# A graph layer that sorts its edges: GpSimd's gathers in another order, and three smaller edits

## The chip, the cores and the metric

The kernel runs on one core of a Trainium2 chip. The metric is device time in microseconds (us), the median of three timed runs of one launch. TensorE (PE), VectorE (DVE), ScalarE (ACT), GpSimd (POOL) and SyncE (SP) each run their own instruction stream in order and wait for one another by semaphores.

## The reference

One GraphSAGE layer over N = 12500 nodes with D = 64 features and E = 800000 random edges:

```python
nsum = _segment_sum(x[src], dst, N)
h_neigh = nsum * deg_inv[:, None]
return x @ w_self + h_neigh @ w_neigh
```

Every edge adds the feature row of its source node to its destination node; the sums are scaled per node and go through two 64x64 matrices.

## The kernel before, in words

The kernel doesn't gather 800000 feature rows. It sorts the edges by a key made of a destination group and a source group, and lets TensorE do gather and scatter with one-hot matrices.

**Keys and first sort.** Each of the 128 partitions takes 6250 edges, packs source and destination into one 32-bit key (`make_keys`) and sorts its run with a comb sort (`sort_runs`). A stage is a DVE minimum and a DVE maximum over pairs (L229), and ACT copies the elements that have no partner (L231). The first stages run over the whole run, the last 36 in three pieces, low, middle and high, so that the low part of each run is final first.

**Features.** Beside the sort `prepare` loads the features `x` (98 blocks of 64 per partition, 6272 values), takes their largest magnitude (`y`, L527 on ACT, L529 on DVE), derives a power of two from it through a small chain on DVE and PE (`e`, `ei`, `sc`, `scl`), and splits each scaled feature into a high part in 16 bits (`xh[..0]`, L552) and a low part (`xh[..1]`: the difference on DVE, L553, and its scaling on ACT, L554). `self_terms` multiplies the features with `w_self` (`xs`, `os`). This code is put in order by a scheduler; what follows stands in program order (`manual_schedule` in `after_sort`).

**Redistribution.** The 128 runs have to be cut at key boundaries and brought to 128 rows of a second level, in two parts (0 and 1). `find_rows` counts in each run how many keys lie below each row's first key: one instruction per row, on ACT (L374) or on DVE (L376). From the counts come start indices `ix`, and `gather_runs` has POOL issue one indirect DMA per run (`u<-d,ix`, L393), each followed by one (part 0) or two (part 1) short memsets of `pad` (`pause`, L306). Each row then holds 128 short sorted runs, and `merge_runs` merges them: first the near stages inside blocks of 32 runs (L415 the first stage of a block, L455 the others, L420 the copies on ACT; the tuple `blocks` says which blocks share an instruction), then `joined` and the far stages over all of them. Block 3 needs the last 32 gathers.

**Windows.** `find_and_gather` counts in the merged rows (L599, L601), and POOL gathers one window of each bucket (`v<-d,ix`, L605); `decode_buckets` turns the windows into source numbers (`sl`, through memory) and destination numbers (`dlT`). Edges that no window holds are leftovers: `leftovers` makes lists of them, and later `uses` says from which block on each list is due.

**Tiles.** 7644 buckets ("blocks") are summed, 8 per tile, 74 tiles per group of output nodes (`OCT` = 6 node blocks of 98 buckets, 588 blocks). For each tile PE does 8 matmuls `ct<-xh,ohs` (L852, gather by one-hot), ACT or DVE copies `ct` to `xg` (L862, L860), and PE does 16 matmuls `acc<-ohd,xg` (L907, scatter by one-hot). DVE makes the one-hots for 28 blocks at a time (`ohs` L823, `ohd` L826), some tiles ahead of PE. A leftover list takes an indirect DMA on POOL (`lx<-xt,lsrc`, L871, five buffers), a one-hot on DVE (`ohl`, L879) and a matmul into `acc` (L887); `rest` issues the DMA up to 160 blocks ahead.

**What is woven in.** Part 1 follows behind part 0. Its 128 run gathers are spread: 64 (`FIRST`) during the merges of part 0, 32 (up to `THEN`) at the end of `sums_and_merge`'s slots, and the last 32 (`runs`) one at every second tile. Its near merges run from tile 8 on, its block 3 and far stages from tile `RESUME` = 80 on, at a pace of 420 ns (`PACE`) per tile; all of them stand in DVE's order between the one-hots. POOL's order mixes the run gathers, the `lx` gathers and the output DMAs (L978) as the tiles come.

Of the kernel before, what the change touches and what calls it, by code (L numbers as in the profile page):

```python
# [22 lines left out]
NB = 98  # L23
# [21 lines left out]
EDGE = 32  # L45
PAUSE = (1, 2)
FIRST = 64
THEN = 96
EXT = 31
SIDE = H + EXT  # L50
# [3 lines left out]
BIG = float(np.array(BIGBITS, np.uint32).view(np.float32))  # L54
SIG = 5.5
AHEAD = 44
RESUME = 80
PACE = 420
SHARE = 503
SHARED = 60  # L60
# [200 lines left out]
class Kernel:  # L261
# [242 lines left out]
    def prepare(self, xp, mps):  # L504
# [19 lines left out]
        nc.sync.dma_start(dg[fd:fd + 1, :N - fd * FB], self.I["deg_inv"][fd * FB:].unsqueeze(0))  # L524

        y = xp.tile([128, NB, D], F32, name="y")
        nc.scalar.activation(y, x, AF.Abs)  # L527
        m = xp.tile([128, 1], F32, name="m")
        nc.vector.tensor_reduce(m, y.rearrange("p b f -> p (b f)"), axis=mybir.AxisListType.X, op=OP.max)  # L529
        ps = mps.tile([128, 128], F32, name="mps", tag="ct", bufs=3)  # L530
        nc.tensor.transpose(ps[:1], m, self.idf)
        e = xp.tile([1, 1], F32, name="e")
# [20 lines left out]
        nc.vector.scalar_tensor_tensor(y, x, scl[:, :1], self.xh[:, :, 0], op0=OP.mult, op1=OP.subtract)  # L553
        nc.scalar.activation(self.xh[:, :, 1], y, AF.Copy, scale=2048.0)  # L554
        nc.sync.dma_start(self.xt.rearrange("(b p) f -> p b f", p=128), self.xh.rearrange("p b a f -> p b (a f)"))

        nc.scalar.activation(y, x, AF.Abs, scale=scl[:, :1])
        z = xp.tile([128, NB, D], BF, name="z")
# [236 lines left out]
    def uses(self):  # L795


        out = []
        for o in range(0, NBID, OCT * NB):
            end = min(o + OCT * NB, NBID)  # L800
            here = []
            for p in range(2):
                for c in range(64):
                    lo = max(o, BASE[p] + c * 2 * KPRS[p])
                    hi = min(end, BASE[p] + (c + 1) * 2 * KPRS[p])
                    if hi > lo:
                        here.append([max(hi + 56, 380 + 24 * c) if p == 0 else hi + 56, p, c, lo // NB, (hi - 1) // NB])
            at = end + 8
            for use in sorted(here)[::-1]:
                at = use[0] = min(use[0], at - 24)  # L810
            out += sorted(here)
        return out
# [16 lines left out]
    def nodes(self, pool, aps, mps):  # L829
# [34 lines left out]

        def rest(b0):

            if len(picked) < self.used + 5 and len(picked) < len(uses) and uses[len(picked)][0] - 160 <= b0 \
                    and uses[len(picked)][1] in self.left:
                _, p, c, _, _ = uses[len(picked)]
                x = pool.tile([128, 128], FH, name="lx", bufs=5)  # L870
                nc.gpsimd.indirect_dma_start(  # L871
                    out=x, out_offset=None, in_=self.xt,
                    in_offset=bass.IndirectOffsetOnAxis(ap=self.left[p][1][:, c:c + 1], axis=0))
                picked.append(x)
                self.picked = len(done)
            if len(ohl) < len(picked) and len(ohl) < self.used + 5 and uses[len(ohl)][0] - 96 <= b0:
                _, p, c, first, end = uses[len(ohl)]
                m = pool.tile([128, 4 * HN], FH, name="ohl", bufs=5)
                nc.vector.tensor_scalar(m[:, :(end + 1 - first) * 2 * HN], self.wide[:, :(end + 1 - first) * 2 * HN],  # L879
                                        self.left[p][0][:, c:c + 1], -float(first * 2 * HN),  # L880
                                        op0=OP.subtract, op1=OP.is_equal)
                ohl.append(m)
            while self.used < len(uses) and uses[self.used][0] <= b0:
                _, p, c, first, end = uses[self.used]
                m = ohl[self.used].rearrange("p (b h n) -> p b h n", h=2, n=HN)
                for h in range(2):
                    nc.tensor.matmul(acc[h][:, first % OCT * HN:(first % OCT + end + 1 - first) * HN],  # L887
                                     picked[self.used], m[:, :end + 1 - first, h], start=False, stop=False)
                self.used += 1
# [167 lines left out]
    def after_sort(self, es, mps, aps):  # L1057
# [5 lines left out]
        with tc.manual_schedule():  # L1063
# [22 lines left out]
            sync.dma_start(self.d1[1], self.runs[:, UPPER1:])  # L1086
            self.l1ab.close()
            rows = self.find_rows(1, mps)
            for _ in range(SHARED):
                next(rows)  # L1090
            ways = None
            for i, _ in enumerate(self.merge_runs(0, u0, other, ((0, 2), (2, 1), (3, 1)))):
                if rows and [next(rows, None) for _ in range(2 - i % 2)][-1] is None:
                    rows = None
                    self.l1b.close()
                    self.gather_runs(1, u1, range(FIRST))
# [8 lines left out]
                    next(ways, None)  # L1105
            for _ in ways:
                pass
            self.store_rows(1, sync)
            self.sums_and_merge(es, mps, aps, u1, other, l2, l2b, l2a, va, vp)

    def sums_and_merge(self, es, mps, aps, u1, other, l2, l2b, l2a, va, vp):
# [11 lines left out]
        for slot in range(at[-1] + 2):  # L1123
            t += SLOT
            if ways and next(ways, None) is None:
                ways = None
                self.gather_runs(1, u1, range(FIRST, THEN))
            if slot < KPRS[0] - NLOWER and not on_act2(0, NLOWER + slot):
                t -= 750
            if slot in at or slot - 1 in at:  # L1130
# [16 lines left out]
        for n in self.nodes(fin, aps, mps):  # L1147
            if left and n >= left_at:
# [4 lines left out]
                        self.check(fin, mps)  # L1153
                else:
                    left_at = n + wait
            if runs and n % 2:
                self.gather_runs(1, u1, [runs.pop(0)])
            if tail and n % 2:
                next(tail, None)
# [55 lines left out]
```

## Time and profile before

| | |
|---|---|
| median of 3 timed runs | 1911.4 us (1903.02 to 1920.62) |
| the profiled execution's own time | 1896.69 us |
| its span, first to last instruction | 1895.0 us |
| busy: DVE, ACT, PE, POOL | 1677.9, 1166.8, 962.2, 841.8 us |
| first tile's one-hots on DVE | from 806.25 us on |

The profile is of one execution. Busy times are shares of one span, but the kernel has stages with different limits, so the stages are read one by one: the sort (to about 348 us), the gathers of part 0 (to about 552 us), its merges and windows (to about 806 us), and the tiles. In a row of the timeline the first number is the start, the second the duration; brackets hold the idle time of the engine before it and what ended it. A row of the windows view has a stretch, its length, and the busy time and count of the chosen instructions.

### The profile page before, as it was taken

How to read it: one execution, taken by the hardware profiler on the slowest of the kernel's cores; microseconds unless marked ns; L12 is line 12 of the kernel's file. 1: busy time of each engine (PE TensorE's matmuls, PEld its weight loads, DVE VectorE, ACT ScalarE, POOL GpSimd, SP SyncE). 2: the span in 40 equal slices, each digit the busy share in tenths (PEclk: the TensorE clock that was granted, in tenths of full speed). 3: DMA queues.
4: the chain of work that ended last, by engine and by line, in shares of the span. 5: the costliest groups of instructions: out<-in, count | busy, mean ns of one | idle time of the engine just before them, and what ended most of it. 6: DMA issues, size and time to landing. Idle time of an engine off the chain costs nothing.

```text
span 1895.0 us, 54521 instructions
## 1 busy us (share of the span) xinstructions
PE 962.2 (51%) x23659; PEld 838.7 (44%) x23659; DVE 1677.9 (89%) x1778; ACT 1166.8 (62%) x1835; POOL 841.8 (44%) x917
## 2 busy tenths in 40 slices
PE   0033000000000000083788887988979999889987
PEld 0023000000000000073677776777768788778886
DVE  7999999997749999795699999998998898888885
ACT  7463019305510022574689888988988887788786
POOL 1000000599889984798737322204662232322421
PEclk9985555555555555587899999999999999999998
DMA  4322000001100012274577877779867888888874
GB/s 152 70 63 73 0 24 8 25 20 52 22 20 10 10 38 70 82 283 137 185 230 246 256 244 251 251 258 312 285 223 250 270 276 257 269 272 278 272 252 147
DMA packets 104804, 305.24 MB, mean 161 GB/s; under 512 B 52945, under 2 KB 60491, under 8 KB 103915
## 3 DMA queue, kind: packets, MB, share of 16 engines
q1 hardware_dynamic: 86347, 277.44, 41.5%
q0 software_dynamic: 17632, 22.17, 8.7%
q8 instruction: 187, 3.06, 0.6%
q10 hardware_dynamic: 576, 2.07, 0.3%
q14 instruction: 62, 0.51, 0.1%
HBM read 282.20 MB, written 19.41 MB: 159 GB/s over the span
## 4 chain that ended last, share of the span: by engine, by line
DVE 40%; PE 24%; POOL 18%; issue 11%; DMA 3%; ACT 3%; DVEq 0%; SPq 0%; ACTq 0%; POOLq 0%
DVE u L455 14%; PE ct L852 13%; POOL u L393 13%; PE acc L907 9%; DVE a L229 7%; DVE b L229 7%; DVE ohd L826 5%; DVE ohs L823 4%; POOL pad L306 3%; POOL lx L871 2%; ACT xg L862 2%; DMA slb<-sl 1%; PE po L970 1%; DMA rd<-dst 1%; PE acc L887 1%
## 5 line engine op out<-in xcount | busy, mean ns | idle before, releaser
L862 ACT ACTIVATE xg<-ct 128x1024 f16<-128x1024 f32 (+1 forms) x898 | 856.4, 1043 | 188.6 <-PE ct L852 167.1
L852 PE MATMUL ct<-xh,ohs 128*128 128x128 f16 x7644 | 540.3, 224 | 69.7 <-DVE ohs L823 36.2
L852 PEld LDWEIGHTS <-ohs 128*128 128x128 f16 x7644 | 449.4, 100 | 110.0 <-issue 51.3
L393 POOL DMA_INDIRECT u<-d,ix x256 | 369.4, 1443 | 217.0 <-DVE ix L385 175.3
L907 PE MATMUL acc<-ohd,xg 64*128 64x80 f16 x15288 | 399.9, 200 | 58.9 <-issue 40.5
L455 DVE TENSOR_TENSOR u<-u 128x1456 f32<-128x1456 f32 (+46 forms) x292 | 394.5, 1378 | 6.6
L871 POOL DMA_INDIRECT lx<-xt,lsrc x140 | 265.6, 1897 | 249.1 <-PE acc L887 213.1
L907 PEld LDWEIGHTS <-xg 64*128 64x128 f16 x15288 | 318.4, 96 | 126.2 <-issue 57.4
L826 DVE TENSOR_TENSOR ohd<-iota,dlT 128x2240 f16<-128x2240 bf16 x273 | 360.3, 1320 | 0.0
L823 DVE TENSOR_SCALAR ohs<-slb,pidx 128x3584 f16<-128x3584 bf16 x273 | 314.6, 1152 | 37.4 <-PE ct L852 25.7
L383 PE MATMUL stp<-idf,st 128*128 128x128 f32 x2 | 0.9, 446 | 356.7 <-DVE st L381 356.7
L229 DVE TENSOR_TENSOR a<-b 128x608 f32<-128x608 f32 (+44 forms) x124 | 173.9, 1445 | 4.6
L229 DVE TENSOR_TENSOR b<-a 128x608 f32<-128x608 f32 (+44 forms) x124 | 173.9, 1444 | 4.3
L978 POOL DMA_DIRECT2D out<-o x25 | 22.8, 913 | 319.7 <-DVE o L977 245.5
L383 PEld LDWEIGHTS stp<-idf,st 128*128 128x128 f32 x2 | 0.4, 182 | 357.2 <-issue 357.2
L662 PE MATMUL tr<-idb,l 128*128 128x128 bf16 x60 | 8.0, 273 | 262.2 <-ACT l L656 258.1
L860 DVE CAST xg<-ct 128x1024 f16<-128x1024 f32 x64 | 78.3, 1223 | 57.6 <-PE ct L852 57.1
L662 PEld LDWEIGHTS <-l 128*128 128x128 bf16 x60 | 5.0, 117 | 265.5 <-ACT l L656 260.8
L420 ACT ACTIVATE u<-u 128x30 f32<-128x30 f32 (+34 forms) x136 | 30.7, 278 | 134.8 <-DVE u L455 73.0
L231 ACT ACTIVATE b<-a 128x1 f32<-128x1 f32 (+21 forms) x52 | 18.7, 379 | 135.5 <-DVE a L229 130.4
L605 POOL DMA_INDIRECT v<-d,ix x60 | 75.4, 1257 | 59.6 <-ACT ix L623 47.4
L374 ACT ACTIVATE junka<-b,c 128x132 bf16<-128x132 f32 (+46 forms) x205 | 90.6, 442 | 11.8 <-DVE b L229 5.9
(153 smaller groups left out, 798.6 us busy)
## 6 DMA issues: line engine op xcount, KB each, us to landing
slb<-sl SPq DMA_DIRECT2D x273, 896.0 KB
u<-d,ix POOLq DMA_INDIRECT x256
xt<-xh SPq DMA_DIRECT2D x1, 3136.0 KB
fo<-own SPq DMA_DIRECT2D x26, 120.0 KB
own<-os SPq DMA_DIRECT2D x12, 256.0 KB
out<-o POOLq DMA_DIRECT2D x24, 120.0 KB
lx<-xt,lsrc POOLq DMA_INDIRECT x140
rd<-dst SPq DMA_DIRECT2D x4, 521.0 KB
```

Source lines behind the costliest of these rows:

```text
L229: nc.vector.tensor_tensor(view(dst, lo + sh, [[st, g], [1, l]]), x, y, op=op)
L374: nc.scalar.activation(junks[0][:, :n], w, AF.Sign, bias=self.c1[:, 0, c:c + 1], accum_out=a)
L393: nc.gpsimd.indirect_dma_start(out=u[:nr, EDGE + p * w:EDGE + (p + 1) * w], out_offset=None, in_=src, in_offset=bass.IndirectOffsetOnAxis( ...
L455: nc.vector.tensor_tensor(view(dst, EDGE + o + out, d), view(src, EDGE + o + x, d), view(src, EDGE + o + x + gap, d), op=op)
L605: self.nc.gpsimd.indirect_dma_start(out=self.v[:, k].bitcast(F32), out_offset=None, in_=flat(self.d2[home(part, k)], 128 * PITCH2[home(par ...
L823: nc.vector.tensor_scalar(s.rearrange("p c s -> p (c s)"), b, self.pidx[:, :1], None, op0=OP.is_equal)
L826: nc.vector.tensor_tensor(d, self.iota[:, None].to_broadcast([128, 14, HN, 2]), ix, op=OP.is_equal)
L852: nc.tensor.matmul(ct[:, i * 128:(i + 1) * 128], cols[i][0], self.xh[:, (b0 + i) % NB].rearrange("p a f -> p (a f)"), start=True, stop=True)
L860: nc.vector.tensor_copy(xg[:, :cnt * 128], ct[:, :cnt * 128])
L862: nc.scalar.activation(xg[:, :cnt * 128], ct[:, :cnt * 128], AF.Copy)
L871: nc.gpsimd.indirect_dma_start(out=x, out_offset=None, in_=self.xt, in_offset=bass.IndirectOffsetOnAxis(ap=self.left[p][1][:, c:c + 1], ax ...
L907: nc.tensor.matmul(acc[h][:, db % OCT * HN:(db % OCT + 1) * HN], xg[r, i * 128:(i + 1) * 128], d[r], start=db % OCT == 0 and sb == 0, stop ...
```

## The change

Seven edits:

- The largest magnitude is taken from 16-bit magnitudes `z` by four DVE maxima of halves (`fold`) and a reduction over 392 values.
- The low parts are made by PE: per 8 blocks, `x` times a scaled identity `by`, minus `xh[..0]` times the identity (`less`), in PSUM, and ACT scales that into `xh`.
- In part 0 the blocks of 32 runs are merged singly from the start (`((0, 1), (1, 1), (2, 1), (3, 1))`), and the row counts of part 1, of which 60 stood ahead of the merges, follow two by two after each merge instruction.
- 7 run gathers of part 1 (`FIRST` to `MORE` = 71) move ahead of the second set of window gathers.
- The last 32 run gathers come at every third tile, and `RESUME` is 100.
- In the first group of nodes all leftover lists are due near the group's end, and their `lx` gathers may be issued up to 400 blocks ahead.

```diff
-RESUME = 80
+RESUME = 100
...
+MORE = 71
...
         y = xp.tile([128, NB, D], F32, name="y")
-        nc.scalar.activation(y, x, AF.Abs)
+        z = xp.tile([128, NB, D], BF, name="z")
+        nc.scalar.activation(z, x, AF.Abs)
+        most, n = z.rearrange("p b f -> p (b f)"), NB * D
+        fold = xp.tile([128, n // 2], BF, name="fold")
+        while n > 512:
+            n //= 2
+            nc.vector.tensor_tensor(fold[:, :n], most[:, :n], most[:, n:2 * n], op=OP.max)
+            most = fold
         m = xp.tile([128, 1], F32, name="m")
-        nc.vector.tensor_reduce(m, y.rearrange("p b f -> p (b f)"), axis=mybir.AxisListType.X, op=OP.max)
+        nc.vector.tensor_reduce(m, fold[:, :n], axis=mybir.AxisListType.X, op=OP.max)
...
         nc.scalar.activation(self.xh[:, :, 0], x, AF.Copy, scale=scl[:, :1])
-        nc.vector.scalar_tensor_tensor(y, x, scl[:, :1], self.xh[:, :, 0], op0=OP.mult, op1=OP.subtract)
-        nc.scalar.activation(self.xh[:, :, 1], y, AF.Copy, scale=2048.0)
+        by = xp.tile([128, 128], F32, name="by")
+        nc.scalar.activation(by, self.idf, AF.Copy, scale=scl[:, :1])
+        less = xp.tile([128, 128], FH, name="less")
+        nc.scalar.activation(less, self.idf, AF.Copy, scale=-1.0)
+        for b0 in range(0, NB, 8):
+            nb = min(8, NB - b0)
+            ps = mps.tile([128, 8, D], F32, name="low", tag="ct", bufs=3)
+            nc.tensor.matmul(ps[:, :nb], by, x[:, b0:b0 + nb], start=True, stop=False)
+            nc.tensor.matmul(ps[:, :nb], less, self.xh[:, b0:b0 + nb, 0], start=False, stop=True)
+            nc.scalar.activation(self.xh[:, b0:b0 + nb, 1], ps[:, :nb], AF.Copy, scale=2048.0)
...
-                        here.append([max(hi + 56, 380 + 24 * c) if p == 0 else hi + 56, p, c, lo // NB, (hi - 1) // NB])
+                        here.append([end if o == 0 else hi + 56, p, c, lo // NB, (hi - 1) // NB])
...
-            if len(picked) < self.used + 5 and len(picked) < len(uses) and uses[len(picked)][0] - 160 <= b0 \
+            early = 400 if b0 < OCT * NB - 160 else 160
+            if len(picked) < self.used + 5 and len(picked) < len(uses) and uses[len(picked)][0] - early <= b0 \
...
-            for _ in range(SHARED):
-                next(rows)
             ways = None
-            for i, _ in enumerate(self.merge_runs(0, u0, other, ((0, 2), (2, 1), (3, 1)))):
-                if rows and [next(rows, None) for _ in range(2 - i % 2)][-1] is None:
+            for i, _ in enumerate(self.merge_runs(0, u0, other, ((0, 1), (1, 1), (2, 1), (3, 1)))):
+                if rows and [next(rows, None) for _ in range(2)][-1] is None:
...
+            self.gather_runs(1, u1, range(FIRST, MORE))
...
-                self.gather_runs(1, u1, range(FIRST, THEN))
+                self.gather_runs(1, u1, range(MORE, THEN))
...
-            if runs and n % 2:
+            if runs and n % 3 == 0:
                 self.gather_runs(1, u1, [runs.pop(0)])
```

How the order moves at three places. First DVE, in the sort, where the maximum `m` is taken (`a`, `b` are the two sort buffers; L229 before and L230 after are the same line). Before:

```order
L229 TENSOR_TENSOR b<-a 128x2449 x2
L529 TENSOR_REDUCE m<-y 128x1
L229 TENSOR_TENSOR a<-b 128x2639 x2
L533 TENSOR_REDUCE e<-mps 1x1
L229 TENSOR_TENSOR b<-a 128x2638 x2
L535 TENSOR_SCALAR ei<-e 1x1
```

And now:

```order
L230 TENSOR_TENSOR b<-a 128x2449 x2
L534 TENSOR_TENSOR fold<-z 128x3136
L230 TENSOR_TENSOR a<-b 128x2639 x2
L534 TENSOR_TENSOR fold<-fold 128x1568
L230 TENSOR_TENSOR b<-a 128x2638 x2
L534 TENSOR_TENSOR fold<-fold 128x784
L230 TENSOR_TENSOR a<-b 128x2775 x2
L534 TENSOR_TENSOR fold<-fold 128x392
L230 TENSOR_TENSOR b<-a 128x2774 x2
L537 TENSOR_REDUCE m<-fold 128x1
```

The five short instructions stand between sort stages, and `m` and all that hangs on it come four stages later. Second ACT, where the features are split, a little later in the sort (L231, now L232, are the sort's copies; `z,s` are passes that count zeros and small values). Before:

```order
L557 ACTIVATE y<-x,scl 128x6272
L231 ACTIVATE b<-a 128x183 x2
L586 ACTIVATE os<-pw 128x512
L581 ACTIVATE xs<-xt 128x512
L562 ACTIVATE z,s_353<-y 128x6272
L231 ACTIVATE a<-b 128x131 x2
```

And now:

```order
L573 ACTIVATE y<-x,scl 128x6272
L232 ACTIVATE b<-a 128x132 x2
L558 ACTIVATE w2n<-wn,part 128x64
L570 ACTIVATE xh<-low 128x8x64 x2
L577 ACTIVATE z,s_412<-y 128x6272
L570 ACTIVATE xh<-low 128x8x64
L232 ACTIVATE a<-b 128x94
L570 ACTIVATE xh<-low 128x8x64 x2
L232 ACTIVATE b<-a 128x95
L578 ACTIVATE z,s_413<-y,lim 128x6272
```

The two long passes `z,s` moved from the stages with 131 and 132 copied elements to those with 94 and 68. Third POOL, where the first leftover gathers `lx` stand in the tile stage (`u` are run gathers of part 1). Before, with 47 run gathers between the last window gather and the first of these rows:

```order
L871 DMA lx<-xt,lsrc_2726 128x128
L393 DMA u<-d_1_61,ix_1468 128x48
L306 MEMSET pad 128x95 x2
L871 DMA lx<-xt,lsrc_2726 128x128
L393 DMA u<-d_1_61,ix_1468 128x48
L306 MEMSET pad 128x95 x2
```

And now, with 30 run gathers ahead of them:

```order
L887 DMA lx<-xt,lsrc_2825 128x128 x2
L394 DMA u<-d_1_61,ix_1561 128x48
L307 MEMSET pad 128x95 x2
L887 DMA lx<-xt,lsrc_2825 128x128 x2
L394 DMA u<-d_1_61,ix_1561 128x48
L307 MEMSET pad 128x95 x2
L887 DMA lx<-xt,lsrc_2825 128x128
```

The first five `lx` moved ahead by 17 run gathers; behind them twelve run gathers follow without an `lx` between.

More of the change, by code (lines that the diff above doesn't have):

```diff
@@ L552, in prepare @@
         nc.scalar.activation(self.xh[:, :, 0], x, AF.Copy, scale=scl[:, :1])
-        nc.vector.scalar_tensor_tensor(y, x, scl[:, :1], self.xh[:, :, 0], op0=OP.mult, op1=OP.subtract)
-        nc.scalar.activation(self.xh[:, :, 1], y, AF.Copy, scale=2048.0)
+        by = xp.tile([128, 128], F32, name="by")
[8 more added lines that the diff above has]
+            nc.scalar.activation(self.xh[:, b0:b0 + nb, 1], ps[:, :nb], AF.Copy, scale=2048.0)
         nc.sync.dma_start(self.xt.rearrange("(b p) f -> p b f", p=128), self.xh.rearrange("p b a f -> p b (a f)"))
         nc.scalar.activation(y, x, AF.Abs, scale=scl[:, :1])
-        z = xp.tile([128, NB, D], BF, name="z")
         s = [xp.tile([128, 1], F32, name=f"s{i}") for i in range(2)]
```

## The prediction

> **What bounds the kernel now.** I read the page first: its engine rows over 40 slices of 47.4 us, and the shares of the chain of waits.
>
> ```profile
> PE   0033000000000000083788887988979999889987
> DVE  7999999997749999795699999998998898888885
> ...
> POOL 1000000599889984798737322204662232322421
> ...
> DVE 40%; PE 24%; POOL 18%; issue 11%; DMA 3%; ACT 3%; DVEq 0%; SPq 0%; ACTq 0%; POOLq 0%
> ```
>
> DVE is full in the sort (slices 1 to 8). In slices 9 to 11 it has holes while POOL is full: POOL's run gathers bound that stretch. Slices 12 to 15 are DVE's merges. Slice 17 opens the tiles, and in slice 18 PE falls to 3 and DVE to 5. So I asked the windows view what DVE and PE did around there, and the waits from 806 to 941.6 us for the cause.
>
> ```profile
> 868.70:941.60 72.90, 36.45 (x44) 0.73 0.44 138
> 941.60:1270.00 328.40, 327.77 (x307) 0.98 0.78 247
> ...
> 806.00:864.60 58.60, 49.63 (x1188) 0.91 0.75 274
> 1270.00:1895.00 625.00, 550.99 (x14139) 0.96 0.80 259
> ```
>
> ```profile
> PE acc L887 <- DMA lx<-xt,lsrc: 37.6, 4, 26.5
> ```
>
> The first two window rows are DVE, the last two PE. PE stood 37.6 us for leftover gathers, and DVE, whose `ohl` buffers PE holds, lost 72.90 - 36.45 = 36.4 us. Then DVE is the bound without a break to 1270 us (327.77 of 328.40), as long as part 1's merges stand between the one-hots. Behind that PE sets the pace: a tile has 8 + 16 = 24 matmuls, 14139 of them are 589 tiles, 1.06 us each. Before the stall it was 1188/24 = 49.5 tiles in 58.6 us, 1.18 us each.
>
> **POOL's pace.** The same view for L393 alone (stretch, length, busy, count):
>
> ```profile
> 429.80:452.30 22.50, 16.21 (x18) 0.50 0.28 91
> 452.30:493.90 41.60, 33.55 (x23) 0.50 0.08 18
> 493.90:505.60 11.70, 8.56 (x9) 0.50 0.12 25
> 505.60:529.60 24.00, 19.13 (x14) 0.50 0.10 20
> 785.70:807.60 21.90, 13.84 (x12) 0.50 0.32 104
> 807.60:868.10 60.50, 45.29 (x23) 0.92 0.74 272
> 868.10:887.00 18.90, 11.80 (x12) 0.50 0.21 65
> ```
>
> A gather with its pause takes 1.25 to 1.30 us beside row counts or an idle DVE (rows 1 and 3), 1.81 beside two-block merges, 1.71 beside single-block ones. In the tiles it is 1.83 at first, 2.63 us beside a full DVE and 1.57 while DVE stands.
>
> **The sort.** DVE loses two long instructions:
>
> ```profile
> 75.90 6.68 DVE L529 TENSOR_REDUCE m<-y 128x1 f32<-128x6272 f32 x1
> 118.76 6.74 DVE L553 SCALAR_TENSOR_TENSOR y<-x,scl,xh 128x6272 f32<-128x6272 f32 x1
> ...
> L826 DVE TENSOR_TENSOR ohd<-iota,dlT 128x2240 f16<-128x2240 bf16 x273 | 360.3, 1320 | 0.0
> ```
>
> Together 13.42 us, both on the chain. The four `fold` maxima handle 5880 values of 16 bits; L826, the nearest 16-bit row, has 1320/2240 = 0.59 ns a value, so 3.5 us, and 0.4 for the reduction over 392 (6.68/6272 each). Net -9.5 us. If `fold` ran like the sort's fp32 pairs (4.57 us for 2130 + 2035 values below, 1.1 ns), it would be 3 us less.
>
> ACT gives some back. The maximum now comes four stages later, and with it ACT's long passes fall where stages are shorter.
>
> ```profile
> 130.87 0.58 ACT L586 ACTIVATE os<-pw 128x512 f32<-128x512 f32 x1
> ...
> 138.71 5.45 ACT L562 ACTIVATE z<-y 128x6272 bf16<-128x6272 f32 x1
> ...
> 151.48 4.57 DVE L229 TENSOR_TENSOR a<-b 128x2130 f32<-128x2130 f32 x2
> ```
>
> Beginning with the 2130 stage ACT has, in order, the copy that opens it, `w2n`, two `low`, the 5.45 us pass with its accumulator read, one more `low`, and only then the copy of 94 elements that the next stage needs. At 0.6 us a `low`, as wide as the 0.58 us copy out of PSUM above, that is about 8 us against 4.57: DVE waits 3.3 us. The second pass (L563) has two stages to hide in. Later three `low` wait for PE, which makes them one by one in three buffers: 1 us more as an estimate from stages of some 4 us. I take 4.2; the bounds are 0 (copies land in time) and 8. PE's own work there is covered by a PE that the first row shows idle. **Sort: -5.3 us.**
>
> **Gathers of part 0.** POOL issues the same 128 gathers, and only the last 32 gate block 3. DVE's earlier start on block 0 is no gain by itself, since DVE stands before block 3 for them:
>
> ```profile
> 552.08 3.32 DVE L415 TENSOR_TENSOR u<-u 128x928 f32<-128x928 f32 x2 [22.75 <-DMA u<-d,ix]
> ```
>
> What counts is POOL's pace. Two single blocks at 24.0 - 14 x 1.30 = 5.8 us of delay each are 11.6 us, the pair now costs 41.6 - 23 x 1.30 = 11.7. The counts between them ran beside gathers at 1.25. So 0, from -11.7 (counts hide all the delay) to +31 (below). ACT's counts, up to four behind a stage now, may delay block 2 by these 22.75 us before anything is late.
>
> The Trainium skill bears on this, "SBUF — State Buffer", section "Who interferes with whom": a DVE instruction in a two-port mode shuts GpSimd out for its whole length, the accumulating form of `tensor_scalar` never does, and a `tensor_tensor` with two SBUF inputs holds up only GpSimd instructions that read SBUF; descriptor generation it infers to be free of it. The trace agrees on the counts (1.25 us a gather) and not on the inference (1.81 beside merges). By the inference merges would cost the gathers nothing and this term is 0 as well.
>
> **Seven gathers moved.** POOL stands before the second set of window gathers:
>
> ```profile
> 698.76 2.02 POOL L393 DMA_INDIRECT u<-d,ix  x1 [0.16 <-issue]
> ...
> 733.34 0.95 POOL L605 DMA_INDIRECT v<-d,ix  x1 [0.30 <-issue]
> 753.63 0.98 POOL L605 DMA_INDIRECT v<-d,ix  x1 [19.34 <-ACT ix L623]
> ```
>
> Seven at 2.6 us (2.02, two memsets of 0.43 together, 0.15) are 18.2, into a hole of 19.34 us. Behind them stand 19 window gathers, for which DVE's decoding waits. +0.5 us, from 0 to 5 if they overrun.
>
> **The tiles.** Up to the stall DVE's order is unchanged, so POOL's times may be read off the rows before: the 31st run gather started at 856.65, and there the first `lx` now stands instead of the 48th place:
>
> ```profile
> 856.65 1.35 POOL L393 DMA_INDIRECT u<-d,ix  x1 [0.15 <-issue]
> ...
> 887.74 0.95 POOL L871 DMA_INDIRECT lx<-xt,lsrc  x1 [0.96 <-issue]
> ...
> 891.13 0.32 PE L887 MATMUL acc<-ohl,lx 128*128 128x80 f16 x2 [26.53 <-DMA lx<-xt,lsrc]
> ```
>
> An `lx` lands 3.4 us after its start (887.74 to 891.13). PE came to the first use at 864.6; this use is now 3 tiles later, near 868, and the next follow every 3 tiles. Five `lx` at 1.9 us (an estimate: 0.95 above, 0.3 between, and some of a busy DVE's delay) and two run gathers at 2.63 fill 856.65 to 871.5: all five are in time. The sixth stands behind twelve more run gathers; its use is 18 tiles behind the old first one, near 886. By 890, when DVE runs dry as it did 4 us into the old stall, seven of the twelve are out at 2.63; five at 1.57 end at 898, and PE goes on at 901: a stall of 15 us instead of 37.6, with DVE idle for 11.
>
> From there to the last run gather POOL has 13 run gathers (2.1, between 1.57 and 2.63), 7 `lx` (1.6) and an output: 40 us, landing near 940. DVE gets to block 3 after its 36.4 us of old work, 11 idle, and five one-hot pairs at PE's pace (17.5 tiles x 1.06 = 18.5): 868.7 + 66 = 934.6, and waits some 5 us. So block 3 begins at 940 against
>
> ```profile
> 941.68 1.39 DVE L415 TENSOR_TENSOR u<-u 128x656 f32<-128x656 f32 x1 [1.09 <-issue]
> ```
>
> but four one-hot pairs, 14 tiles, are further on. DVE's saturated stretch then has the same length, and 14 tiles fewer follow at 1.06 us: -1.7 - 14.9 = **-17 us**. Bounds: -31 (no idle but 5 us) and 0 (next part). Part 1's last buckets are decoded 14 tiles later, at tile 508, needed at 592: covered.
>
> **Sum.** -5.3 + 0 + 0.5 - 17 = -22 us: 1896.7 becomes 1875 for a profiled execution. That execution was 14.7 us below the median of the timed runs, so I put the difference on the median: **1889 us**.
>
> **Rivals.**
> - *The stall only moves.* If POOL keeps 2.63 to the end, the 25 run gathers and 8 `lx` behind 871.5 take 82 us, block 3 starts past 954 and DVE, in order, waits there. The 14 tiles are paid back: tile term about -2, 1904 us. For it: nothing lets DVE rest but the stall itself. Against: 1.57 whenever it does.
> - *Shorter holds.* Each merge instruction of blocks 0 and 1 is half as long and a count follows it, so a gather waits for one short instruction. Of 11.7 us 8 go: 1881. For it: 1.25 beside counts. Against: 1.71 beside single blocks already.
> - *Starvation, the slower side.* With a count between each minimum and maximum DVE no longer pauses for its own results, and an unbroken DVE has held a gather for 31.9 us:
>
> ```profile
> 1001.71 31.90 POOL L871 DMA_INDIRECT lx<-xt,lsrc  x1 [8.05 <-PE acc L887]
> ```
>
>   If no gather gets through in the 30 counted steps (some 43 us, 24 gathers at 1.30), the gather chain grows by 31 us: 1920; over blocks 0 and 1 it is 51 us and 1940. It makes the kernel slower once more than 17 gathers (22 us) are held. Against: the counts' own row.
> - *No effect*: DVE's hole in the tiles may be filled anyhow. Then 1911; the 36.4 us speak against it.
>
> **How the numbers follow.** The forecast 0.52 (own range 1879 to 1899), the moved stall 0.20, shorter holds 0.16, starvation 0.08, no effect 0.04. The range, 1868 to 1908, takes in the tile and ACT bounds on both sides and leaves out starvation. One per cent, about what a measurement can tell here, is 1892.3: six tenths of the forecast, nearly all of the shorter holds and a little of the rest make 0.52 for faster; most of starvation, and an unnamed loss, 0.10 for slower; 0.38 between.
>
> **What would show it.** L529 and L553 gone and part 0's first gather near 342 instead of 347.8 us; a DVE wait of some 3 us for ACT in the 2035 stage; first to last gather of part 0 still about 204 us; no wait of L887's successor above 1 us for the first five `lx`, one of about 15 at the sixth; block 3 of part 1 within 10 us of the last run gather. I am wrong if the gathers between 430 and 500 us leave 1.8 us a piece, or if the run gathers end past 950.

## The result and the profile after

The changed kernel takes 1892.45 us (median of 6 runs, 1886.9 to 1897.11), the kernel before 1913.24 (median of 6, 1903.02 to 1920.62): a ratio of 0.9886 with a 95% interval of 0.9855 to 0.9918, some 21 us. The profiled execution of the changed kernel took 1888.32 us, its span is 1886.6. Beside the profiled execution before, that is only 8.4 us less. The two comparisons disagree; second profiles of both kernels, further down, say why.

The page after, PE and DVE over 40 slices, and the shares of the chain of waits:

```profile
PE   0015100000000000185888888888868989988997
DVE  6999999999559999797799999998897888888885
...
DVE 42%; PE 25%; POOL 13%; issue 10%; ACT 5%; DMA 4%; DVEq 0%; SPq 0%; ACTq 0%; POOLq 0%
```

The `3` of PE and the `56` of DVE, where the tiles had stalled, are now `5` and `77`: the hole is smaller, not gone. POOL's share of the chain fell from 18% to 13%. PE has a small `151` near the start, the matmuls of the low parts.

**The sort**, timeline of the changed kernel: POOL's first gather of part 0, DVE's 2035 stage, and ACT ahead of it (start, length, engine, line, operation, idle time before and what ended it):

```profile
340.61 1.02 POOL L394 DMA_INDIRECT u<-d,ix  x1 [135.39 <-DVE ix L386]
```

```profile
148.99 4.38 DVE L230 TENSOR_TENSOR b<-a 128x2035 f32<-128x2035 f32 x2 [2.28 <-ACT a L232]
```

```profile
142.76 5.45 ACT L577 ACTIVATE z<-y 128x6272 bf16<-128x6272 f32 x1
...
148.18 0.61 ACT L570 ACTIVATE xh<-low 128x512 f16<-128x512 f32 x1
148.66 0.31 ACT L232 ACTIVATE a<-b 128x94 f32<-128x94 f32 x1
```

DVE stands 2.28 us for the copy of 94 elements, which ACT reaches only behind the 5.45 us pass and one `low`. The copies out of PSUM that wait for PE later (1.35, 0.96 and twice 0.48 us) hold no sort stage. The first gather starts at 340.61 us instead of 347.79.

**The gathers of part 0.** DVE comes to block 3 of part 0 here:

```profile
542.19 3.32 DVE L416 TENSOR_TENSOR u<-u 128x928 f32<-128x928 f32 x2 [22.13 <-DMA u<-d,ix]
```

From the first gather that is 201.58 us, against 552.08 - 347.79 = 204.29 before.

**The tiles.** PE's one long wait for a leftover gather, what DVE and ACT do behind it, and DVE's start of block 3 of part 1:

```profile
888.92 0.45 PE L903 MATMUL acc<-ohl,lx 128*128 128x160 f16 x2 [14.88 <-DMA lx<-xt,lsrc]
```

```profile
891.61 1.02 ACT L877 ACTIVATE xg<-ct 128x1024 f16<-128x1024 f32 x1 [14.39 <-PE ct L867]
892.53 0.23 ACT L421 ACTIVATE u<-u 128x36 f32<-128x36 f32 x1
```

```profile
892.79 0.69 DVE L456 TENSOR_TENSOR u<-u 128x510 f32<-128x510 f32 x1 [11.03 <-ACT u L421]
```

```profile
931.90 1.28 DVE L416 TENSOR_TENSOR u<-u 128x656 f32<-128x656 f32 x1 [3.75 <-DMA lx<-xt,lsrc]
```

PE's wait reaches DVE by way of ACT: ACT stands 14.39 us for a tile's `ct`, the merges' copy `u` stands behind it in ACT's order, and DVE's next merge waits 11.03 us for that copy.

To compare positions behind this point I number DVE's `ohd` instructions from 0. Each makes the destination one-hots of 28 blocks, 3.5 tiles, and comes with one `ohs`, so I call them pairs (the expectations below say "one-hot"). Pair 160 is behind the merges and all decoding in every kernel, before:

```profile
1469.55 1.32 DVE L826 TENSOR_TENSOR ohd<-iota,dlT 128x2240 f16<-128x2240 bf16 x1
```

and after:

```profile
1452.51 1.32 DVE L841 TENSOR_TENSOR ohd<-iota,dlT 128x2240 f16<-128x2240 bf16 x1
```

So the changed kernel is 17.0 us ahead at pair 160. Of these only 6.5 are left at the last pair (1868.96 against 1875.47). Two questions follow. Where did the tiles lose before pair 160, where block 3 had begun 9.8 us early with four pairs already made? And is the loss behind pair 160 the change's?

**A new wait in the decoding.** SP's queue, 1375 to 1480 us, first before and then after (line, what it waited for: us in total, times, longest):

```profile
SPq L821 <- DVE ohs L823: 88.6, 26, 7.3
SPq L821 <- DMA slb<-sl: 2.2, 2, 1.2
SPq L954 <- DVE ohl L879: 1.4, 1, 1.4
```

```profile
SPq L836 <- DVE ohs L838: 73.0, 21, 6.7
SPq L970 <- DVE o L993: 11.4, 1, 11.4
```

L970 is the load of an output's own term (`fo<-own`, L954 before). Its pool has two buffers. In the new order the tail's output, the group's two outputs and the decoding meet, so the third load stands until DVE's add at L993 has used up a buffer. SP works in order, and the `slb` transfers that feed the one-hots stand behind it:

```profile
1410.47 0.36 SPq L970 DMA_DIRECT2D fo<-own  x1
1414.34 0.32 SPq L836 DMA_DIRECT2D slb<-sl  x1
1428.45 0.39 SPq L970 DMA_DIRECT2D fo<-own  x1
1428.89 6.95 SPq L836 DMA_DIRECT2D slb<-sl  x4
```

Between 1414.7 and 1428.4 us SP issues nothing. The delay reaches DVE and then PE. Of the waits between `flag`, which DVE writes when the decoding ends (1416.01), and pair 160, these two stand in the changed kernel and have no counterpart in the kernel before:

```profile
DVE ohs L838 <- DMA slb<-sl: 3.7, 2, 2.3
PE ct L867 <- DVE xg L875: 2.7, 1, 2.7
```

DVE waits for `slb`, its cast of `xg` comes late, and PE waits for the cast.

### The profile page after: what moved, and what is told of

Its sections match the earlier page's. It is cut to its first block, busy times and chain, and to the rows that moved or that the text cites. A ratio compares the mean times of both kernels' runs of the same rounds, so it can differ in the third digit from the quotient of the medians.

```text
span 1886.6 us, 54681 instructions
## 1 busy us (share of the span) xinstructions
PE 980.7 (52%) x23698; PEld 839.0 (44%) x23698; DVE 1667.2 (88%) x1805; ACT 1169.7 (62%) x1868; POOL 809.9 (43%) x917
## 4 chain that ended last, share of the span: by engine, by line
DVE 42%; PE 25%; POOL 13%; issue 10%; ACT 5%; DMA 4%; DVEq 0%; SPq 0%; ACTq 0%; POOLq 0%
DVE u L456 15%; PE ct L867 13%; POOL u L394 10%; PE acc L923 9%; DVE b L230 6%; DVE a L230 6%; DVE ohd L841 6%; DVE ohs L838 4%; DMA slb<-sl 2%; ACT xg L877 2%; POOL pad L307 2%; POOL lx L887 1%; DVE u L416 1%; PE acc L903 1%; POOL v L620 1%
## 5 line engine op out<-in xcount | busy, mean ns | idle before, releaser
L394 POOL DMA_INDIRECT u<-d,ix x256 | 374.0, 1461 | 178.8 <-DVE ix L386 135.4
L923 PE MATMUL acc<-ohd,xg 64*128 64x80 f16 x15288 | 405.9, 199 | 64.2 <-issue 48.9
L456 DVE TENSOR_TENSOR u<-u 128x1456 f32<-128x1456 f32 (+51 forms) x314 | 398.1, 1291 | 19.7 <-ACT u L421 13.6
L887 POOL DMA_INDIRECT lx<-xt,lsrc x140 | 231.2, 1652 | 261.6 <-PE acc L903 228.4
L230 DVE TENSOR_TENSOR b<-a 128x608 f32<-128x608 f32 (+44 forms) x124 | 173.8, 1444 | 6.3 <-ACT a L232 2.3
L230 DVE TENSOR_TENSOR a<-b 128x608 f32<-128x608 f32 (+44 forms) x124 | 173.9, 1445 | 4.5
L421 ACT ACTIVATE u<-u 128x96 f32<-128x96 f32 (+36 forms) x155 | 32.9, 258 | 134.3 <-DVE u L456 71.1
L232 ACT ACTIVATE b<-a 128x1 f32<-128x1 f32 (+21 forms) x52 | 18.7, 379 | 128.1 <-DVE a L230 122.2
```

Of the source, the lines that this page charges most:

```text
L230: nc.vector.tensor_tensor(view(dst, lo + sh, [[st, g], [1, l]]), x, y, op=op)
L394: nc.gpsimd.indirect_dma_start(out=u[:nr, EDGE + p * w:EDGE + (p + 1) * w], out_offset=None, in_=src, in_offset=bass.IndirectOffsetOnAxis( ...
L456: nc.vector.tensor_tensor(view(dst, EDGE + o + out, d), view(src, EDGE + o + x, d), view(src, EDGE + o + x + gap, d), op=op)
L887: nc.gpsimd.indirect_dma_start(out=x, out_offset=None, in_=self.xt, in_offset=bass.IndirectOffsetOnAxis(ap=self.left[p][1][:, c:c + 1], ax ...
L923: nc.tensor.matmul(acc[h][:, db % OCT * HN:(db % OCT + 1) * HN], xg[r, i * 128:(i + 1) * 128], d[r], start=db % OCT == 0 and sb == 0, stop ...
```

## The experiments

Ratios are to the kernel before on the same chip, with 95% intervals.

### Each part alone

`sort_alone` is the kernel before with only the edits in `prepare`; `counts_alone` has only `((0, 1), (1, 1), (2, 1), (3, 1))` with two row counts per merge step and none ahead; `tiles_alone` has only GpSimd's order:

```diff
# tiles_alone, on the kernel before
+MORE = 71
-RESUME = 80
+RESUME = 100
-                        here.append([max(hi + 56, 380 + 24 * c) if p == 0 else hi + 56, p, c, lo // NB, (hi - 1) // NB])
+                        here.append([end if o == 0 else hi + 56, p, c, lo // NB, (hi - 1) // NB])
+            early = 400 if b0 < OCT * NB - 160 else 160
-            if runs and n % 2:
+            if runs and n % 3 == 0:
```

> Only the edits in prepare (folded maximum in 16 bits, low parts by TensorE); the rest is the kernel before. Theory: the whole chain starts earlier and nothing gives it back. First gather of part 0 near 340.6 us instead of 347.8, block 3 of part 0 near 545, first one-hot near 800, ratio to the kernel before 0.996 (-7 us). Rival, the gain is absorbed: DVE or PE only waits longer later (for POOL's gathers, the leftovers or the last tiles), ratio 1.000. Rival of size: without the change of the tiles the stall there grows by the 7 us, first one-hot near 800 but block 3 of part 1 still near 941.

> Only the merge order of part 0 (single blocks 0 to 3) with two row counts before each merge step, none ahead of it. Theory: the gathers of part 0 take about 2.7 us less from first to last, as in the changed kernel (201.6 us from the first one to block 3 instead of 204.3); first gather stays at 347.8, block 3 near 549, ratio 0.9985. Rival, starvation: a DVE without pauses holds the gathers, block 3 near 583, ratio 1.016. Rival, shorter holds: block 3 near 544, ratio 0.996.

> Only GpSimd's order: seven run gathers moved ahead, first leftover gathers early, run gathers every third tile, merges of part 1 resumed at step 100. Sort and part 0 as before. Theory, the late loss belongs to the order: one-hot 24 comes some 18 us earlier than before, and still does at one-hot 144, then 10 to 12 us are lost between one-hots 144 and 160 (75 us there instead of 62.5), so the end is 5 to 8 us earlier, ratio 0.996. Rival, the late loss is that one execution's: one-hots 144 to 160 in 62 to 66 us, the end some 17 us earlier, ratio 0.991. Rival, the stall only moves: block 3 of part 1 more than 10 us later than before, ratio 0.999.

Measured: 0.9941 (0.9917 to 0.9965), 0.9972 (0.9951 to 0.9993) and 0.9955 (0.9932 to 0.9978). Their product is 0.9869, inside the interval of the whole change: the parts add up within that interval, and no absorption is seen. In the traces `sort_alone` has its first gather at 340.17 us and `counts_alone` needs 201.14 us to block 3, both as expected. The time of `sort_alone` fell by more than its trace explains (0.9941 is 11 us, the trace shows 6 to 8); that stays open, though the 0.996 that was expected lies inside the interval. Its block 3 of part 1 came at 936.67, 5 us before the first profile of the kernel before and level with the second (936.95, below), so whether the stall in the tiles takes back a part of the gain is not shown. `tiles_alone` was 21.0 us ahead at pair 32, 22.2 at pair 144 and 6.3 at pair 160. It repeated the late loss, so that loss belongs to the new order and not to one execution. (A part of the early lead is only borrowed: four pairs more stand ahead of merges and decoding that are still to come.) The rival that only moves the stall fell: block 3 came 2.8 us earlier, not 10 later.

### The late loss: casts or SP's queue

```diff
# share_later, on the changed kernel
-SHARE = 503
+SHARE = 517
```

> The changed kernel with one number more changed: VectorE takes its half of the casts of xg from tile 517 on instead of 503, as far behind the decoding of part 1 as it stood in the kernel before. Theory S: in the changed kernel the casts fall into the decoding, so the 12 us lost between one-hots 144 and 160 come from them: that stretch falls from 74.8 us to 63 to 67 and the time to some 8 us under the changed kernel's, ratio to the kernel before near 0.984. Rival Q: SP stands 11.4 us behind an output's own-term load, and the slb transfers behind it come late; that stays: the stretch remains at 72 to 75 us and the ratio at 0.988 to 0.989.

Measured: 0.9882 (0.9845 to 0.9919), pairs 144 to 160 in 74.4 us. Theory S fell: moving DVE's casts out of the decoding gives nothing that can be seen, and SP's wait stayed, at 13.9 us.

```diff
# fo_three, on the changed kernel; tiles_fo is the same on tiles_alone
-        own = pool.tile([FB, 4, D], F32, name="fo", bufs=2)
+        own = pool.tile([FB, 4, D], F32, name="fo", bufs=3)
```

> The changed kernel with three buffers for fo instead of two. Theory Q: SP's load of fo stood 11.4 us (13.9 in two other kernels with the new order) for the output add that frees a buffer, and the slb transfers behind it came late. With a third buffer that wait goes, no DMA hole of 14 us at 1414 to 1428, and one-hots 144 to 160 take 63 to 68 us instead of 74.8; the end comes 7 to 11 us earlier, ratio to the kernel before 0.983 to 0.985. Rival, the wait covers nothing (slb is three ahead, DVE and PE waited for it only 3.7 and 2.7 us; the decoding itself costs the 12 us): the stretch stays at 71 to 75 us, ratio 0.987 to 0.989.

> The kernel with GpSimd's new order alone (sort and part 0 as before) and three buffers for fo. Theory Q: one-hots 144 to 160 fall from 78.3 us to 63 to 68, and the order alone is then worth about 17 us instead of 8: ratio 0.990 to 0.992. Rival as above: 74 to 78 us, ratio 0.9955.

Measured: 0.9845 (0.9816 to 0.9873) and 0.9917 (0.9887 to 0.9947), 0.0041 and 0.0038 below the same kernels with two buffers. Either difference alone lies within the intervals; that both came out alike makes some 7 us likely. SP's wait for the add is gone in `fo_three`:

```profile
SPq L836 <- DVE ohs L838: 89.4, 25, 8.2
SPq L836 <- DMA slb<-sl: 2.8, 2, 1.6
SPq L1211 <- DVE ohl L895: 1.2, 1, 1.2
```

But the stretch from pair 144 to 160 took 73.0 and 72.1 us, not 63 to 68. The times came out as theory Q had them, the stretch did not. The stretch was a bad ruler: decoding ends near pair 148 in the old order and near 152 in the new, so the new order has more of it between pairs 144 and 160. A better one starts where the decoding ends, at `flag` (L990, L1006). Before, the 12 pairs from there to pair 160 took 46.2 us, 3.85 each. In the changed kernel 8 pairs took 36.5 us, in `fo_three` 33.3; in `tiles_alone` 40.1, in `tiles_fo` 33.2. At 3.85 a pair 8 would take 30.8. But pairs are DVE's work, and PE does not keep a fixed distance from them. The view counts PE's matmuls `ct`, 8 to a tile, in these stretches (the kernel before, the changed one, `fo_three`; busy time and count of PE, DVE and ACT):

```profile
1423.38:1469.55 46.17, 26.01 (x372) 7.34 (x6) 37.69 (x40) 0.96 0.75 257
```

```profile
1416.01:1452.51 36.50, 18.89 (x253) 4.88 (x4) 25.16 (x26) 0.91 0.64 210
```

```profile
1415.17:1448.47 33.30, 18.51 (x264) 4.89 (x4) 26.44 (x28) 0.95 0.70 245
```

That is 46.5, 31.6 and 33 tiles, or 0.99, 1.15 and 1.01 us each; `tiles_alone` has 262 in 40.07 us (1.22), `tiles_fo` 264 in 33.22 (1.01). At 0.99 a tile the two-buffer kernels lose 5.1 and 7.6 us, the three-buffer ones 0.5 each. So SP's wait costs 4.6 and 7.1 us here, of the size of the 7 us in the times, and almost nothing else is lost. The waits say the same. In all six kernels with the new order and two buffers DVE's `ohs` stands 3.0 to 4.9 us for `slb` in this stretch and PE 2.1 to 3.2 us for DVE's cast; no profile with three buffers and none with the old order has either wait. The granted clock in the stretch is 0.84 to 0.91 in five of the six and 1.00 in `lx8`, which loses least (34.2 us).

### Does the stall at the sixth `lx` matter, and does the early issue?

```diff
# lx8, on the changed kernel
-            if len(picked) < self.used + 5 and len(picked) < len(uses) and uses[len(picked)][0] - early <= b0 \
+            if len(picked) < self.used + 8 and len(picked) < len(uses) and uses[len(picked)][0] - early <= b0 \
-                x = pool.tile([128, 128], FH, name="lx", bufs=5)
+                x = pool.tile([128, 128], FH, name="lx", bufs=8)
# (ohl likewise)
# no_early, on the changed kernel
-            early = 400 if b0 < OCT * NB - 160 else 160
+            early = 160
```

> The changed kernel with eight buffers for lx and ohl instead of five, so that the sixth to eighth leftover gather go ahead of nine run gathers. Theory P, GpSimd's queue bounds the stretch: PE's wait of 14.9 us at the sixth lx goes and DVE doesn't stand for it, but the run gathers come later (more of them beside a busy DVE) and DVE stands before block 3 instead, 10 to 20 us in place of 3.8; block 3 of part 1 at 930 to 940 us (931.9 in the changed kernel), ratio 0.987 to 0.991. Rival, the wait at the sixth lx is what is lost: block 3 near 918 to 922, ratio near 0.981.

> The changed kernel with the leftover gathers of the first group issued 160 steps ahead of their use as before, not 400; every third tile a run gather, seven moved ahead and step 100 stay. Only GpSimd's order differs. Theory P: PE waits some 14 us at the first lx instead of at the sixth, little at the sixth, and block 3 of part 1 comes within 4 us of 931.9; ratio 0.987 to 0.990. Rival, the early issue earned the gain: PE stands 25 us or more in all for lx, block 3 near 945, ratio near 0.995.

`lx8` came to 0.9932 (0.9901 to 0.9964), `no_early` to 0.9886 (0.9855 to 0.9918). PE's waits for `lx` and DVE's block 3 in `lx8`:

```profile
900.81 0.32 PE L903 MATMUL acc<-ohl,lx 128*128 128x80 f16 x2 [5.75 <-DMA lx<-xt,lsrc]
914.25 0.31 PE L903 MATMUL acc<-ohl,lx 128*128 128x80 f16 x2 [4.22 <-DMA lx<-xt,lsrc]
```

```profile
931.92 1.29 DVE L416 TENSOR_TENSOR u<-u 128x656 f32<-128x656 f32 x1 [8.78 <-DMA u<-d,ix]
```

and in `no_early`:

```profile
864.49 0.31 PE L903 MATMUL acc<-ohl,lx 128*128 128x80 f16 x2 [10.96 <-DMA lx<-xt,lsrc]
...
889.71 0.45 PE L903 MATMUL acc<-ohl,lx 128*128 128x160 f16 x2 [7.45 <-DMA lx<-xt,lsrc]
```

```profile
928.45 1.28 DVE L416 TENSOR_TENSOR u<-u 128x656 f32<-128x656 f32 x1 [5.94 <-DMA lx<-xt,lsrc]
```

The 14.88 us wait can be cut up, put off or split between the first `lx` and the sixth, and block 3 still begins between 928 and 932 us. Four profiles whose order is the same up to there (the changed kernel twice, `share_later`, `fo_three`) put it between 925.8 and 931.9, so smaller differences can't be read. Theory P held for block 3, with DVE's wait in `lx8` a little shorter than expected (8.8, not 10 to 20), and PE's in `no_early` less wholly at the first `lx` (10.96 and 7.45 us, not some 14 and little). The ratio of `lx8` lies above both expectations: up to pair 160 it is level with the changed kernel (1452.61 and 1452.51), behind it its profile has the longest stretch of all (423.7 us), and why its runs were slower is not shown. Within these few microseconds GpSimd's queue as a whole bounds the stretch to block 3: which of its gathers come first decides only who waits. The early issue brings nothing that can be seen. What is left of the edits to the tiles is above all that merges resume at step 100, so that four pairs more are made while DVE would wait for the gathers anyway; neither this step nor the spacing of one run gather in three tiles was run alone.

### Is the tail behind pair 160 the change's?

> The kernel before once more, for a second profile of it. Theory V: from one-hot 160 to the last one PE sets the pace and its own pauses without a wait differ from execution to execution (407.5 to 423.7 us in nine profiles of kernels that share this code, mean 415); the 405.9 of the first profile was at the short end, so this one takes 408 to 424 there, while the times up to one-hot 160 repeat within 3 us (block 3 of part 1 near 942, one-hot 160 near 1470). Rival: the kernel before really has a shorter tail: 404 to 407.

> The changed kernel once more. Theory V: up to one-hot 160 it repeats within 5 us (1452.5; the place of the sixth lx may move block 3 by some us, 926 to 932), behind it 408 to 424 us. Rival, the tail is longer because of the change: 416 to 417 again, where the kernel before has 406.

The second profile of the kernel before took 1910.44 us, that of the changed kernel 1889.05: 21.4 us apart, as the medians are. The windows from pair 160 to the last pair (stretch, length, busy time and count of PE, PEld, DVE, ACT, POOL, granted clock, DMA share, GB/s), before, first and second profile:

```profile
1469.55:1875.47 405.92, 369.18 (x9601) 326.19 (x9594) 346.35 (x374) 328.75 (x358) 126.97 (x82) 0.97 0.84 266
```

```profile
1474.46:1890.90 416.44, 372.52 (x9646) 326.75 (x9643) 346.70 (x374) 330.98 (x360) 122.65 (x82) 0.98 0.81 259
```

and the changed kernel:

```profile
1452.51:1868.96 416.45, 377.33 (x9669) 330.18 (x9666) 346.99 (x374) 331.42 (x362) 120.29 (x82) 0.97 0.82 260
```

```profile
1456.23:1869.58 413.35, 373.74 (x9667) 326.95 (x9665) 346.64 (x374) 331.31 (x362) 122.57 (x82) 0.98 0.83 262
```

Theory V's range held for the tail: the first profile of the kernel before was simply short there, and that is most of why its execution lay 16.5 us under the median of six. Its reason did not hold in this pair: PE's pauses without a wait come to 32.8 and 32.5 us in the two profiles, and PE's waits for ACT and DVE are what grew, from under 4 to some 11 us. Nor did the times hold to 3 us before pair 160: 4.7 us came off ahead of block 3, and 9.3 were added between block 3 and `flag`. Over all profiles this shared code gives 405.9 to 417.7 us in the old order and 409.2 to 423.7 in the new; the two can't be told apart.

### Single blocks or counts between, and a version that uses what was found

```diff
# singles_only, on the kernel before
-            for i, _ in enumerate(self.merge_runs(0, u0, other, ((0, 2), (2, 1), (3, 1)))):
+            for i, _ in enumerate(self.merge_runs(0, u0, other, ((0, 1), (1, 1), (2, 1), (3, 1)))):
# more_72_resume_104, on fo_three
-MORE = 71
+MORE = 72
-RESUME = 100
+RESUME = 104
```

> The kernel before with part 0's first two blocks merged one at a time, and the row counts left as they were (60 ahead of the merges, then two and one in turn). Theory, shorter holds: the single blocks alone bring the gain of the gathers, 201 to 202.5 us from the first gather to block 3 (204.3 before, 201.4 with the counts moved too). Rival, the counts between bring it: 203.5 to 205 us.

> The changed kernel with the third fo buffer, one more run gather moved ahead (eight in all, 2.4 us into a hole of 2.9) and merges of part 1 resumed at step 104. Theory: DVE's wait of 6.9 us before block 3 (the kernel with three fo buffers) is filled by one more pair of one-hots, and one gather less stands in the tiles: one-hot 160 some 3 us earlier, 1445, ratio to the kernel before 0.981 to 0.984. Rival, nothing is won: more work beside the gathers holds them and block 3 comes as much later, ratio 0.984 to 0.987.

`singles_only` needs 203.44 us from its first gather (346.48) to block 3 (549.92). The five profiles with the old merge order lie at 203.06 to 204.31. The lowest two had gained 1.1 us in their first 48 gathers, ahead of every merge. The stretch from the 61st to the 101st gather, beside the merges, is the better measure: 64.5 us in all five, 63.8 with single blocks alone, 59.7 to 60.4 in the eight profiles with the counts between as well. So single blocks alone bring some 0.7 us, and the rest comes with the counts between. Over the whole stretch to block 3 the gain is some 3 us, because merges and counts that begin earlier cost the gathers ahead of the 61st 1.1 us. A kernel with the counts moved and the pair kept was not run, so what the counts bring without single blocks is not shown.

`more_72_resume_104` took 1873.96 us, 0.9805 (0.9766 to 0.9843), the fastest of all. DVE goes into block 3 without a wait:

```profile
928.71 0.43 DVE L993 TENSOR_TENSOR o<-o,fo 120x256 f32<-120x256 f32 x1
929.09 2.48 DVE L416 TENSOR_TENSOR u<-u 128x656 f32<-128x656 f32 x2
```

and pair 160 comes at 1440.79, 8 us earlier than in `fo_three` (1448.47), where 3 were expected. Two numbers were changed at once; which of them did it is not shown. Its interval overlaps that of `fo_three`, but lies wholly below that of the change as given.

### All profiles side by side

Starts in us, read from each timeline; "b0" is block 3 of part 0 after the first gather, "b3" block 3 of part 1.

| kernel | first gather | b0 | pair 0 | b3 | flag | pair 160 | from there to the last pair |
|---|---|---|---|---|---|---|---|
| before | 347.79 | 204.29 | 807.32 | 941.68 | 1423.38 | 1469.55 | 405.9 |
| before_again | 346.74 | 204.31 | 806.29 | 936.95 | 1427.91 | 1474.46 | 416.4 |
| sort_alone | 340.17 | 204.05 | 799.81 | 936.67 | 1418.02 | 1464.18 | 412.9 |
| counts_alone | 348.02 | 201.14 | 804.36 | 938.37 | 1418.82 | 1469.11 | 407.5 |
| singles_only | 346.48 | 203.44 | 805.05 | 937.76 | 1425.34 | 1471.52 | 417.7 |
| tiles_alone | 348.09 | 203.06 | 805.60 | 938.91 | 1423.15 | 1463.22 | 423.2 |
| tiles_fo | 348.23 | 203.24 | 805.96 | 938.00 | 1424.09 | 1457.31 | 409.2 |
| after | 340.61 | 201.58 | 796.71 | 931.90 | 1416.01 | 1452.51 | 416.5 |
| after_again | 342.03 | 201.10 | 797.57 | 930.39 | 1420.13 | 1456.23 | 413.3 |
| share_later | 340.77 | 201.39 | 796.61 | 925.76 | 1411.12 | 1449.74 | 410.5 |
| lx8 | 342.24 | 201.40 | 798.16 | 931.92 | 1418.39 | 1452.61 | 423.7 |
| no_early | 340.25 | 199.96 | 794.70 | 928.45 | 1408.51 | 1446.66 | 415.1 |
| fo_three | 341.47 | 200.15 | 796.12 | 928.81 | 1415.17 | 1448.47 | 414.7 |
| more_72_resume_104 | 341.45 | 200.82 | 796.74 | 929.09 | 1411.22 | 1440.79 | 412.7 |

## Why the prediction was right, and where a step failed

The forecast of 1889 us and the range held, and the sum of -22 us is close to the measured 21. But three terms came out better than predicted, by 5.2 us together, and the largest worse by 7.1; that the sum still fits is luck. Means over the rows of the table:

- **Sort, predicted -5.3.** Six profiles with the old `prepare` start the first gather at 347.6 us, eight with the new at 341.1: **-6.4**. The mechanism was as described: 13.42 us went, the four maxima and the reduction took 1.78 + 0.97 + 0.56 + 0.35 + 0.55 = 4.2 (3.9 predicted), and ACT held DVE for 2.28 (3.3 predicted). The further 1 us for `low` waiting on PE did not come.
- **Gathers of part 0, predicted 0.** Five old profiles without the new counts need 203.8 us, eight with them 200.9, and `singles_only` 203.4: **-2.9**. Of the two reasons that were weighed, shorter merge instructions bring next to nothing alone (0.7 us beside the merges) and the gain comes with the counts between them, if at a quarter of the 11.7 us that were the bound. The rule of the Trainium skill, "SBUF — State Buffer", section "Who interferes with whom", that the accumulating `tensor_scalar` never shuts GpSimd out, agrees with that. The prediction took the 1.81 us beside merges as against that section's inference on descriptor generation, which is too strong: a run gather reads `ix`, and if that counts, the rule on `tensor_tensor` that the prediction gives beside it would hold the gather up as well. Starvation did not happen: no kernel with the counts took longer.
- **Seven gathers moved, predicted +0.5.** From block 3 of part 0 to pair 0 the kernels with the old order take 255.1 to 255.6 us, those with the new 254.4 to 254.5: **-0.7**. The hole took them.
- **Tiles, predicted -17.** The first half held closely in size: five `lx` in time, 14.88 us at the sixth (15 predicted), DVE idle for 11.03 (11 predicted), block 3 at 3.75 us of wait (5 predicted; the row names the `lx` behind the last run gather). The 11 us came by another path, though: the prediction took them from DVE's wait for `ohl` in the old stall, and the row shows a merge that waits for ACT's copy. From pair 0 to block 3 five old kernels take 133.7 us and eight new ones with step 100 132.8: -0.9 against -1.7. From block 3 to `flag` both orders take 480 to 491. **The step that failed is "four one-hot pairs, 14 tiles, are further on ... 14 tiles fewer follow at 1.06 us", -14.9.** It took the tiles behind the decoding at PE's pace. But the decoding, now 14 tiles later, met the outputs, SP stood 9.9 to 13.9 us in each of the six new kernels with two `fo` buffers, and there a tile took 1.15 and 1.22 us behind the decoding (the changed kernel and `tiles_alone`), not 0.99. From pair 0 to pair 160 these take 655.3 us and five old ones 665.2: **-9.9** for the whole term. With a third buffer it is 651.9, -13.3, and with step 104 and one gather more moved 644.1, -21.1. Half of the shortfall is thus the buffer's; the rest, some 3 us, is within what single profiles differ by (662.2 to 668.2 in the old order). "Part 1's last buckets are decoded 14 tiles later ... covered" looked at when the buckets are needed, and not at what else SP and the output buffers do at that time.

The sum of the terms so measured is -6.4 - 2.9 - 0.7 - 9.9 = -19.9 us, and 20.8 was measured between the medians. Putting the profiled sum on the median by the 14.7 us between them was right: the second profile before, at 1910.44, shows that the first was a short execution. Had the changed kernel's profile been set against the first one alone, the change would seem worth 8 us.

Of the rivals, the moved stall, starvation and no effect fell. Shorter holds had a gain of the right sign and a third of its size; of its two reasons the half length brings nearly nothing by itself, and the gain comes only with the count that follows each merge.

## What to carry to other kernels

Moving work along a schedule moves it past other things that share an in-order queue: look at what that queue (here SP, with two kinds of loads) waits for at the new place, and give a small buffer pool one buffer more before blaming an engine. If one queue as a whole is late, reordering inside it only chooses who waits; giving the waiting engine other work can gain. And compare two kernels at marks inside the trace, behind the work that both have done, before comparing spans, since one profiled execution may be 15 us from the median, as here. A mark must count the work of the engine that sets the pace: pairs of one-hots, DVE's work, hid what tiles, PE's work, showed.

## What the runs showed of the hardware that was not expected

- From pair 160 on, the same work took between 405.9 and 423.7 us in 14 profiles, at a granted clock of 0.96 to 0.98 throughout. PE's pauses in which it waited for nothing that the profile shows came to 31 to 46 us there, up to 3.9 us at a time; `lx8` had the longest tail and the most of them (45.5 us). They are not the whole spread: the two profiles of the kernel before have the same sum of them and are 10.5 us apart. What causes them was not tried.
- While PE had next to nothing to do, from the first gather to block 3, the granted clock is recorded as 0.50 in most profiles and as 1.00 in two (`before_again`, `counts_alone`). That is the record and not the clock, at least where it can be tested, at the first tiles: 24 matmuls `ct` take as long at a recorded 0.50 (the kernel before) as at a recorded 1.00 (`before_again`). In these two profiles the first record of the clock comes at about 820 us, in the others before 152 us. The view of `ct`, PE alone (stretch, length, busy time and count, granted clock, DMA share, GB/s):

```profile
807.51:810.23 2.72, 2.71 (x24) 0.50 0.97 380
```

```profile
806.47:809.19 2.72, 2.72 (x24) 1.00 0.93 369
```
